# Strassen's seven block products for the third of four matrix layers, in a kernel of block attention and two MLPs on one core

## The chip, the core and the metric

The kernel runs on one core of one Trainium2 chip. The core has a matrix engine (TensorE, PE in the profile; PEld are its weight loads), a vector engine (VectorE, DVE), an activation engine (ScalarE, ACT), GpSimd (POOL) and a queue engine (SyncE, SP) that issues the transfers between HBM and SBUF, the on-chip memory of 128 partitions. Matmuls write to PSUM, eight banks of 128 x 512 float32. The metric is device time of one execution in microseconds (us), as the median of several runs.

## The reference

Attention over a band and block summaries gives x of 1536 tokens x 512; a gated MLP and a squared-ReLU MLP follow. The four matrix layers below are 512 x (2 x 1536), 1536 x 512, 512 x 2048 and 2048 x 512; q, k, v are 2 x 8 x 768 x 64.

```python
def reference(**kwargs):
    ...
    attn_out = _attn_ref(**attn_kwargs)
    B, H, S, D = attn_out.shape
    x = np.ascontiguousarray(attn_out.transpose(0, 2, 1, 3)).reshape(B * S, H * D)
    x = _moe_ref(x=x, **moe_kwargs)
    return _moe2_ref(x=x, **moe2_kwargs)

def _moe_ref(x, w_gate, w_val, w_out):
    g = x @ w_gate                          # layer one, with val
    silu = g * (1.0 / (1.0 + np.exp(-g)))
    val = x @ w_val
    return (silu * val @ w_out)             # layer two

def _moe2_ref(x, w_in, w_out):
    h = np.maximum(x @ w_in, 0.0)           # layer three
    return (h * h @ w_out)                  # layer four
```

## The kernel before

**Precision.** Every operand of the four layers is kept as two tiles of the format float32r, a high part (a ScalarE cast) and a low part (VectorE: the value less the high part), and each product is three matmuls, high x high, high x low and low x high (`ORDER`). The weights arrive as float64 words; ScalarE and VectorE convert them to float32 once (`convert`), a float32 copy is kept in HBM (`kept1`, `kept2`, `kept34`), and later passes load that.

**Tiling and stages.** The tokens are cut into 3 sets of 512 (`TS`). After a prologue with the first set's attention, a list of `periods` is worked off in order: 36 periods "12" (3 sets x 12 column tiles of 128 of layer one, each with one tile of layer two), then 48 periods "34" (3 sets x 16 column tiles of layer three, each with one tile of layer four). Period k multiplies the column tile of layer one or three into a bank of `ps_m` (two banks), and behind it `second` does layer two or four for the tile of period k-1, into four banks of `ps_c` that accumulate over a whole set. A period "12" has 24 + 12 matmuls of 512 columns, a period "34" has 12 (L538, `multiply3`: weights stationary, 512 tokens moving) + 12 (L557: 128 tokens of h stationary, 512 columns of the fourth weight moving).

**Work beside it.** In a period "34" ScalarE takes relu (L751) and square (L752), VectorE the square in float32 and the low part (L753, L754); both split the weights of the next period (`split_chunk`, L224 and L225). Attention of sets 1 and 2 is laid into the periods of the sets ahead by hand (`place`, with the tables `first`, `after` and `late`, three steps to a period: step 3k + j). The conversion of the third and fourth weights (`background`) runs in the periods of sets 1 and 2, 7/6 steps of it per step. When a set of layer two is complete, its four banks are split into x2 (L565, L566).

**Order.** All of it is written in program order under a manual schedule: each engine works through its own instructions strictly in that order and waits on semaphores. Buffers come from pools (`x_p`, `h_p`, `t_p`, `wr_p`, `wf_p`, `ws_p`, and `const` and `att_p` for attention); a tile's first writer waits until the buffer's previous tile has been read. SyncE issues the loads in order too.

## Time and profile before

| what | us |
|---|---|
| median of 3 runs (lowest, highest) | 643.67 (643.62, 645.46) |
| the profiled execution, its own time | 643.53 |
| its span, first to last instruction | 641.8 |
| TensorE, VectorE, ScalarE busy in it | 630.0, 427.0, 344.0 |
| the 48 periods "34" and the tail of layer two (373.67 to 637.00) | 263.33 |
| the last set of periods "12" (275.83 to 373.67) | 97.84 |

The span is one profiled execution; the runs are timed without a profile. Busy times are of each engine alone and lie beside each other; matmuls overlap in the records, so that a busy TensorE says nothing yet about the interval between two of them.

### The profile page before, as it was taken

The page shows a single profiled execution, that of the slowest core. Times are in us where ns is not written, and L with a number is a line of the kernel's source. Part 1 is how long each engine was busy: PE and PEld are TensorE (multiplying, and loading weights), DVE is VectorE, ACT ScalarE, POOL GpSimd, SP SyncE. Part 2 cuts the span into 40 slices and gives each one's busy share as a digit, 9 for nine tenths or more (in the row PEclk, how much of TensorE's full clock was granted, in tenths as well). Part 3 has the DMA queues.
Part 4 walks back from the last instruction along what each step waited for, and adds up shares of the span by engine and source line. Part 5 has one row for each costly group of instructions (what it writes and reads, how often), then busy time and mean ns, then how long its engine had stood idle before and what let it go on. Part 6 is the DMA issues. An engine that isn't in the chain of part 4 may idle for free.

```text
span 641.8 us, 8650 instructions
## 1 busy us (share of the span) xinstructions
PE 630.0 (98%) x3176; PEld 515.7 (80%) x3176; DVE 427.0 (67%) x519; ACT 344.0 (54%) x623; POOL 25.8 (4%) x41
## 2 busy tenths in 40 slices
PE   8889999999999999999999999999999999999997
PEld 6657788877888888888888888888888888888885
DVE  5999999997577776777767664444454444544443
ACT  3683877884466887554444344444444444444442
POOL 3411000000000000000000000000000000000000
PEclk9899999999999999999999999999999999999999
DMA  8999999747984965766755333222252222432311
GB/s 341 320 371 369 361 328 357 260 170 242 369 249 128 338 203 203 245 246 234 254 201 189 123 117 113 99 96 96 73 182 92 91 95 99 162 101 99 100 50 65
DMA packets 51995, 125.62 MB, mean 196 GB/s; under 512 B 8304, under 2 KB 15216, under 8 KB 50416
## 3 DMA queue, kind: packets, MB, share of 16 engines
q1 hardware_dynamic: 51952, 125.06, 57.1%
q8 instruction: 25, 0.41, 0.3%
q14 instruction: 18, 0.15, 0.1%
HBM read 103.28 MB, written 20.97 MB: 194 GB/s over the span
## 4 chain that ended last, share of the span: by engine, by line
PE 92%; DVE 4%; ACT 2%; issue 1%; POOL 0%; POOLq 0%; DVEq 0%
PE bank L529 29%; PE bank L557 20%; PE bank L538 20%; PE bank L555 15%; PE bank L362 2%; PE bank L465 2%; PE bank L449 1%; PE bank L277 1%; ACT s L393 1%; PE bank L375 1%; DVE wlo L225 1%; DVE wf L188 1%; DVE ks L346 0%; PE bank L370 0%; DVE m L382 0%
## 5 line engine op out<-in xcount | busy, mean ns | idle before, releaser
L225 DVE TENSOR_TENSOR wlo<-wf,whi 128x1024 fp32r<-128x1024 f32 (+2 forms) x85 | 122.1, 1436 | 48.6 <-ACT whi L224 47.9
L224 ACT CAST whi<-wf 128x1024 fp32r<-128x1024 f32 (+2 forms) x85 | 104.1, 1225 | 79.3 <-PE bank L557 54.2
L529 PE MATMUL bank<-xh,whi 128*128 128x512 f32 x288 | 115.8, 402 | 0.0
L529 PE MATMUL bank<-xh,wlo 128*128 128x512 f32 x288 | 112.8, 392 | 2.1 <-DVE wlo L225 2.1
L529 PE MATMUL bank<-xl,whi 128*128 128x512 f32 x288 | 112.6, 391 | 0.6 <-DVE xl L476 0.6
L753 DVE TENSOR_TENSOR r<-r 128x512 f32<-128x512 f32 x48 | 33.2, 692 | 89.2 <-ACT hh L752 89.2
L751 ACT ACTIVATE r<-bank 128x512 f32<-128x512 f32 x48 | 28.7, 598 | 87.6 <-PE bank L538 87.6
L557 PE MATMUL bank<-whi,hl 128*128 128x512 f32 x192 | 74.8, 390 | 0.0
L557 PE MATMUL bank<-whi,hh 128*128 128x512 f32 x192 | 74.7, 389 | 0.0
L557 PE MATMUL bank<-wlo,hh 128*128 128x512 f32 x192 | 74.7, 389 | 0.0
L538 PE MATMUL bank<-xh,whi 128*128 128x512 f32 x192 | 74.7, 389 | 0.0
L538 PE MATMUL bank<-xl,whi 128*128 128x512 f32 x192 | 74.7, 389 | 0.0
L538 PE MATMUL bank<-xh,wlo 128*128 128x512 f32 x192 | 74.7, 389 | 0.0
L529 PEld LDWEIGHTS bank<-xh,wlo 128*128 128x128 f32 x288 | 54.0, 188 | 14.8 <-DVE wlo L225 3.4
L739 ACT CAST hh<-g 128x512 fp32r<-128x512 f32 x36 | 22.2, 617 | 77.9 <-DVE g L738 77.9
L529 PEld LDWEIGHTS bank<-xh,whi 128*128 128x128 f32 x288 | 54.1, 188 | 12.0 <-ACT g L736 0.7
L529 PEld LDWEIGHTS bank<-xl,whi 128*128 128x128 f32 x288 | 54.1, 188 | 11.8 <-DVE xl L476 1.3
L555 PE MATMUL bank<-hh,whi 128*128 128x512 f32 x144 | 57.2, 397 | 0.0
L555 PE MATMUL bank<-hh,wlo 128*128 128x512 f32 x144 | 56.1, 390 | 0.0
L555 PE MATMUL bank<-hl,whi 128*128 128x512 f32 x144 | 56.1, 389 | 0.0
L557 PEld LDWEIGHTS bank<-whi,hl 128*128 128x128 f32 x192 | 36.0, 188 | 7.8 <-DVE hl L754 0.3
L557 PEld LDWEIGHTS bank<-whi,hh 128*128 128x128 f32 x192 | 36.0, 188 | 7.6
(87 smaller groups left out, 899.4 us busy)
## 6 DMA issues: line engine op xcount, KB each, us to landing
wf<-kept SPq DMA_DIRECT2D x120, 256.0 KB
raw<-in_w_dram SPq DMA_DIRECT2D x44, 512.0 KB
...
```

Source lines behind the costliest of these rows:

```text
L188: nc.vector.scalar_tensor_tensor(out=w, in0=hw, scalar=0xC0000000, in1=w, op0=ALU.bitwise_and, op1=ALU.bitwise_or)
L224: lambda: nc.scalar.copy(hi[:, cs], t),
L225: lambda: nc.vector.tensor_sub(lo[:, cs], t, f32(hi[:, cs])),
L362: nc.tensor.matmul(ps[:, i * W:(i + 1) * W], self.q[:, j * UB + i, :], self.kw[j][:, i, 0:W], start=True, stop=True,)
L465: nc.tensor.matmul(ps[r, at + i * QB:at + (i + 1) * QB], self.v[:, j * UB + i, r], a[:, i * P + h * QB:i * P + (h + 1) * QB], start=True, ...
L529: nc.tensor.matmul(p, w[a][:, c], x[i][kk], start=(kk == 0 and n == 0), stop=(kk == KD - 1 and n == 2),)
L538: nc.tensor.matmul(p, w[a][:, c], x[i][kk], start=(kk == 0 and n == 0), stop=(kk == KD - 1 and n == 2),)
L555: nc.tensor.matmul(ps[t], w[a][:, c], h[e], start=(f == 0 and n == 0), stop=(f == last and n == 2))
L557: nc.tensor.matmul(ps[t], h[e][:, t * P:(t + 1) * P], w[a][:, off:off + DM], start=(f == 0 and n == 0), stop=(f == last and n == 2),)
L739: nc.scalar.copy(h[0], g)
L751: nc.scalar.activation(r, p, ACTF.Relu)
L753: nc.vector.tensor_mul(r, r, r)
```

## The change

Layer three is worked in 2 passes of 768 tokens (`NG`), each with 8 steps (`NB`) of 256 columns of its weight; step p takes two neighbouring column tiles. A step is a product of 2 x 2 blocks: tokens in two halves of 384 (`TB`), the 512 inputs in two halves of 256, the columns in two of 128. It is done by seven products of blocks in Winograd's form of Strassen's method, in place of eight: m1 to m7 (`block(p, n)`), each 2 x 3 matmuls of 384 columns, from four weight sums (`sums34`: t1 to t4) and four token sums (`operands`: s1 to s4 in the usual naming, here `s3`, `a21`, `a21`, `s4`). The sums of products (`u2`, `u3`, `sum_up`) give the four blocks of the output; `sum_up` squares the positive part, `high34` and `low34` split it, and `fourth` multiplies layer four for step p-1 into six banks (four of `ps_c`, two of `ps_a`). The order inside a step alternates products and parts of layer four (`rest(0)` to `rest(3)`); in step 0 the rest is what is left of layer two.

Tokens and weights of the seven products are summed in float32 and then split: x2 stays float32 (`put_x2` copies, nothing is split there). The sums and splits of the first pass's tokens are laid into steps 76 on of the third set of layer one, those of the second pass into steps 1 to 8 of the first (`ready`). The float32 weights of a step are loaded two steps ahead (`load34`). Attention's pools sit at the other end of SBUF and are closed after step 72, and their place becomes `xo_p`; the raw words' pools are closed four steps ahead of layer three and become `wr34`. The conversion of the third and fourth weights runs at 9/7 steps per step.

```diff
+    att_c, raw_c = ExitStack(), ExitStack()
+    const = att_c.enter_context(tc.tile_pool(name="const", bufs=1, side="right"))
+    att_p = att_c.enter_context(tc.tile_pool(name="att", bufs=1, side="right"))
...
+    x_p = ctx.enter_context(tc.tile_pool(name="x", bufs=6))
...
+    wr_p = raw_c.enter_context(tc.tile_pool(name="wr", bufs=3))
+    vn_p = raw_c.enter_context(tc.tile_pool(name="vn", bufs=2))
...
-    def multiply3(p, w, x):
-        for kk in range(KD):
-            c = slice(kk * P, (kk + 1) * P)
-            for n, (a, i) in enumerate(ORDER):
-                nc.tensor.matmul(
-                    p, w[a][:, c], x[i][kk],
-                    start=(kk == 0 and n == 0), stop=(kk == KD - 1 and n == 2),
...
-
...
+
+    def second(f, w, off, h, ts):
...
-        last = (F1 if kind == "12" else F2) - 1
-        for t in range(4):
+            acc[:] = [bank(ps_c) for _ in range(4)]
+        for t in ts:
...
-        for t in range(4):
-            if kind == "12":
-                nc.scalar.copy(x2[0][t], ps[t])
-                nc.vector.tensor_sub(x2[1][t], ps[t], f32(x2[0][t]))
-            else:
...
+                nc.tensor.matmul(acc[t], w[a][:, c], h[e], start=(f == 0 and n == 0), stop=(f == F1 - 1 and n == 2))
...
+    TB = 384
+    HK = KD // 2
+    NG = B * S // (2 * TB)
+    NB = F2 // 2
...
+    def put_x2(i, t):
...
+        pieces.sort(key=lambda p: p[0] - p[1])
+        for copy, (a, e) in zip((nc.scalar.copy, nc.vector.tensor_copy), pieces):
+            n = a // TB
+            if n not in x2:
+                x2[n] = x_p.tile([P, KD, TB], F32, tag="x", name="x2")
+            copy(x2[n][:, t, a - n * TB:e - n * TB], acc[t][:, a - i * TS:e - i * TS])
+
...
+    def operands(g):
+        (a11, a12), (a21, a22) = ([x2[2 * g + t][:, k * HK:(k + 1) * HK, :] for k in range(2)] for t in range(2))
+        d = x_p.tile([P, KD, TB], F32, tag="x", name="dx")
+        s3, s4 = d[:, 0:HK, :], d[:, HK:KD, :]
+
+        def hi(n, src):
+            xo[g, n] = xo_p.tile([P, 2, HK, TB], F32R, tag="o", name="o", bufs=9)
+            nc.scalar.copy(xo[g, n][:, 0, :, :], src)
+
+        def lo(n, src):
+            nc.vector.tensor_sub(xo[g, n][:, 1, :, :], src, f32(xo[g, n][:, 0, :, :]))
+
+        def split(n, src):
+            return [lambda: hi(n, src), lambda: lo(n, src)]
+
+        sub, add = nc.vector.tensor_sub, nc.vector.tensor_add
+        return (
+            split(0, a11)
+            + [lambda: sub(s3, a11, a21), lambda: add(a21, a21, a22)]
+            + split(4, a21)
+            + [lambda: sub(a21, a21, a11), lambda: sub(s4, a12, a21)]
+            + split(5, a21) + split(2, s4) + split(6, s3) + split(3, a22) + split(1, a12)
+        )
+
+    BLK = HK * P
+    OF = (("bb", 0), ("bb", 1), ("b2", 0), ("t4", 1), ("tt", 0), ("tt", 1), ("t4", 0))
...
+    f_34, w3_t, w4_t, h_t = {}, {}, {}, {}
+
+    def load34(p, j):
+        pool, tag = (wr34, "f") if p % 2 and j else (wf_p, "wf")
+        t = f_34[p, j] = pool.tile([P, CC], F32, tag=tag, name="wf")
+        nc.sync.dma_start(out=t[:, 0:2 * C2], in_=kept34[2 * (p % NB) + j][:, :])
+
+    def sums34(p):
+        f1, f2 = f_34[p, 0], f_34[p, 1]
+        b11, b21, b12, b22 = (f[:, k * BLK:(k + 1) * BLK] for f in (f1, f2) for k in range(2))
+        t1, t2, t3, t4 = (f[:, (4 + k) * BLK:(5 + k) * BLK] for f in (f1, f2) for k in range(2))
+        sub = nc.vector.tensor_sub
+        return [lambda: sub(t1, b12, b11), lambda: sub(t2, b22, t1), lambda: sub(t3, b22, b12), lambda: sub(t4, b21, t2)]
+
+    def source34(p, tag):
+        j, a, n = {"bb": (0, 0, 2), "tt": (0, 4, 2), "b2": (1, 1, 1), "t4": (1, 4, 2)}[tag]
+        return f_34[p, j][:, a * BLK:(a + n) * BLK], n * BLK
+
+    def hi3(p, tag):
+        src, n = source34(p, tag)
+        t = w3_t[p, tag] = wr34.tile([P, 2, n], F32R, tag=tag, name=tag, bufs=2 if tag in ("bb", "t4") else 1)
...
+    def lo3(p, tag):
+        src, n = source34(p, tag)
+        t = w3_t[p, tag]
+        nc.vector.tensor_sub(t[:, 1, :], src, f32(t[:, 0, :]))
...
+    def hi4(p, j):
+        if j == 0:
+            w4_t[p] = tuple(ws_p.tile([P, CC], F32R, tag=f"w{e}", name=f"w4{e}") for e in ("hi", "lo"))
...
+    def lo4(p, j):
+        c = slice(j * DM, (j + 1) * DM)
+        nc.vector.tensor_sub(w4_t[p][1][:, c], f_34.pop((p, j))[:, C2:2 * C2], f32(w4_t[p][0][:, c]))
+
+    def block(p, n, pool=ps_m):
+
+        g, (tag, half) = p // NB, OF[n]
+        w, x = w3_t[p, tag], xo[g, n]
+        ps = bank(pool)
+        for k in range(HK):
+            c = slice(half * BLK + k * P, half * BLK + (k + 1) * P)
+            for i, (a, e) in enumerate(ORDER):
+                nc.tensor.matmul(
+                    ps[:, 0:TB], w[:, a, c], x[:, e, k, :], start=(k == 0 and i == 0), stop=(k == HK - 1 and i == 2)
+                )
+        return ps[:, 0:TB]
...
+    def snap(ps, tag):
+        t = part(tag)
+        nc.scalar.copy(t, ps)
+        return t
...
+    def sum_up(a, other):
+        t = t_p.tile([P, TB], F32, tag="t", name="c")
+        nc.vector.tensor_add(t, a, other)
+        nc.vector.scalar_tensor_tensor(out=t, in0=t, scalar=0.0, in1=t, op0=ALU.max, op1=ALU.mult)
+        return t
+
+    def high34(p, n, c):
+        nc.scalar.copy(new_h34(p, n)[:, 0, :], c)
+
+    def low34(p, n, c):
+        nc.vector.tensor_sub(h_t[p, n][:, 1, :], c, f32(h_t[p, n][:, 0, :]))
...
+    def fourth(p, n):
+
+        g, m = divmod(p, NB)
+        if m == 0 and n == 0:
+            acc[:] = [bank(ps_c) for _ in range(4)] + [bank(ps_a) for _ in range(2)]
+        f, t = 1 - n // 2, n % 2
+        h, w = h_t.pop((p, n)), w4_t[p]
+        for j in range(3):
+            for i, (a, e) in enumerate(ORDER):
+                nc.tensor.matmul(
+                    acc[3 * t + j], h[:, e, j * P:(j + 1) * P], w[a][:, f * DM:(f + 1) * DM],
+                    start=(m == 0 and n < 2 and i == 0), stop=(m == NB - 1 and n >= 2 and i == 2),
+                )
...
+        def attention_done():
+            nonlocal xo_p
+            att_c.close()
+            xo_p = ctx.enter_context(tc.tile_pool(name="xo", bufs=1, side="right"))
+            for j, f in enumerate(operands(0)):
+                at(late, 76 + j + j // 3, f)
+
...
+        e = 3 * len(periods)
+        at(first, 6 * F1, attention_done)
+        at(late, e - 6, lambda: load34(0, 0))
+        at(late, e - 4, lambda: load34(0, 1))
+        at(late, e - 4, words_done)
+        at(late, e - 3, lambda: [f() for f in sums34(0)])
+        for n, tag in ((3, "bb"), (3, "tt"), (2, "b2"), (2, "t4")):
+            at(late, e - n, lambda tag=tag: hi3(0, tag))
+            at(late, e - n, lambda tag=tag: lo3(0, tag))
+        at(late, e - 1, lambda: load34(1, 0))
+        at(late, e - 1, lambda: load34(1, 1))
...
-                if F1 <= k < K34:
-                    ticks += 7
-                    while ticks >= 6:
+                if k >= F1:
+                    ticks += 9
+                    while ticks >= 7:
                         next(bg, None)
-                        ticks -= 6
-
...
+        for p in range(NG * NB + 1):
...
+            if live:
+                spare = ps_m if p else ps_a
+                m1, m5 = block(p, 0), block(p, 4)
+                if more:
+                    for f in sums34(p + 1):
+                        f()
+            rest(0)
+            if live:
+                s1, s5 = snap(m1, "s1"), snap(m5, "s5")
+                if p:
+                    high34(p - 1, 2, c2)
+                    low34(p - 1, 2, c2)
+                prepare(0)
+                hi4(p, 0)
+                hi4(p, 1)
+                m6, m7 = block(p, 5, spare), block(p, 6, spare)
+                lo4(p, 0)
+                lo4(p, 1)
+            elif p:
+                high34(p - 1, 2, c2)
+                low34(p - 1, 2, c2)
+            rest(1)
+            if live:
+                u2, u3 = (h_p.tile([P, TB], F32, tag=t, name=n) for t, n in (("hh", "u2"), ("hl", "u3")))
+                nc.vector.tensor_add(u2, m6, s1)
+                nc.vector.tensor_add(u3, m7, u2)
+                nc.vector.tensor_add(u2, u2, s5)
+                if more:
+                    hi3(p + 1, "bb")
+                c = sum_up(u3, s5)
+                high34(p, 1, c)
+                if more:
+                    lo3(p + 1, "bb")
+                low34(p, 1, c)
+                prepare(1)
+                if p == 0:
+                    put_x2(bi, 0)
+                    put_x2(bi, 1)
+                if p + 2 < NG * NB:
+                    load34(p + 2, 0)
+                    load34(p + 2, 1)
+                m3, m4 = block(p, 2), block(p, 3)
+                if more:
+                    hi3(p + 1, "tt")
+                    lo3(p + 1, "tt")
+            rest(2)
+            if live:
+                c = sum_up(m3, u2)
+                high34(p, 0, c)
+                c2 = sum_up(m4, u3)
+                low34(p, 0, c)
+                high34(p, 3, c2)
+                low34(p, 3, c2)
+                prepare(2)
+                if p == 0:
+                    put_x2(bi, 2)
+                    put_x2(bi, 3)
+                m2 = block(p, 1, spare)
+                if more:
+                    hi3(p + 1, "b2")
+                    lo3(p + 1, "b2")
+                    hi3(p + 1, "t4")
+            rest(3)
+            if live:
+                c2 = sum_up(m2, s1)
+                if more:
+                    lo3(p + 1, "t4")
```

Two places show how instructions move. On TensorE, before, the end of a period "34" and the start of the next look like this (`whi`, `wlo` are the two parts of a weight tile, `xh`, `xl` of the tokens, `hh`, `hl` of h):

```order
L538 MATMUL bank_5288<-xh3_3465,whi_5246 128x512
L538 MATMUL bank_5288<-xl3_3469,whi_5246 128x512
L538 MATMUL bank_5288<-xh3_3465,wlo_5247 128x512
L557 MATMUL bank_4801<-whi_5246,hh_5248 128x512
L557 MATMUL bank_4801<-whi_5246,hl_5249 128x512
L557 MATMUL bank_4801<-wlo_5247,hh_5248 128x512
```

In the changed kernel, in the middle of step 5, between two of layer four's parts (`o` is a split token operand, `tt`, `t4`, `b2`, `bb` are split weight blocks or sums, `h34` a split block of h):

```order
L666 MATMUL bank_3609<-w4lo_4065,h34_4103 128x512
L666 MATMUL bank_3610<-w4hi_4064,h34_4103 128x512 x2
L666 MATMUL bank_3610<-w4lo_4065,h34_4103 128x512
L628 MATMUL bank_4258<-o_3093,b2_4156 128x384 x6
L628 MATMUL bank_4265<-o_3202,t4_4159 128x384 x6
L666 MATMUL bank_3605<-w4hi_4064,h34_4208 128x512 x2
L666 MATMUL bank_3605<-w4lo_4065,h34_4208 128x512
```

Where twelve matmuls of 512 columns stood behind twelve of another layer, groups of six with 384 columns stand in ones or twos between groups of nine of layer four.

On VectorE, before, a period "34" is three instructions (here two periods' worth, the weight split `wlo` between square and split of h):

```order
L754 TENSOR_TENSOR hl_5249<-r_5267,hh_5248 128x512
L225 TENSOR_TENSOR wlo_5285<-wf_5226,whi_5284 128x1024
L753 TENSOR_TENSOR r_5303<-r_5303 128x512
L754 TENSOR_TENSOR hl_5287<-r_5303,hh_5286 128x512
L225 TENSOR_TENSOR wlo_5321<-wf_5265,whi_5320 128x512
```

In the changed kernel step 0 begins like this, up to the copies of x2 (`wf` are the loaded weights and their sums, `u2`, `u3` and `c` the sums of products, `bank` a product in PSUM, `s1`, `s5` copies of m1 and m5):

```order
L595 TENSOR_TENSOR wf_3456<-wf_3458,wf_3456 128x256 x2
L595 TENSOR_TENSOR wf_3458<-wf_3458 128x256
L595 TENSOR_TENSOR wf_3458<-wf_3456 128x256
L618 TENSOR_TENSOR w4lo_3489<-wf_3353,w4hi_3488 128x512
L618 TENSOR_TENSOR w4lo_3489<-wf_3384,w4hi_3488 128x512
L932 TENSOR_TENSOR u2_3511<-bank_3492,s1_3484 128x384
L933 TENSOR_TENSOR u3_3512<-bank_3499,u2_3511 128x384
L934 TENSOR_TENSOR u2_3511<-u2_3511,s5_3486 128x384
L647 TENSOR_TENSOR c_3518<-u3_3512,s5_3486 128x384
L648 SCALAR_TENSOR_TENSOR c_3518<-c_3518 128x384
L609 TENSOR_TENSOR bb_3516<-wf_3456,bb_3516 128x512
L655 TENSOR_TENSOR h34_3521<-c_3518,h34_3521 128x384
```

Ahead of the first sum that reads a product, VectorE now has four weight sums and two splits of the fourth weight; behind these three rows of u the sum and square of one block, a weight split and a split of h, and only behind all of it, with the copies of x2 and the split `tt`, the sum that reads m3 and gives its bank back (the next row, `c` from a bank and `u2`).

## Rows read from the trace of the kernel before

Durations in rows of the timeline are us, in grouped rows the last number ahead of the second bar is the mean in ns; a bracket or an arrow names what ended the idle time before.

**Rows 1.** The page, part 1: busy us, share of the span, instructions.

```profile
span 641.8 us, 8650 instructions
...
PE 630.0 (98%) x3176; PEld 515.7 (80%) x3176; DVE 427.0 (67%) x519; ACT 344.0 (54%) x623; POOL 25.8 (4%) x41
```

**Rows 2.** Stretches (us): busy us of each engine (instructions), granted clock, DMA share, GB/s.

```profile
275.83:373.67 97.84, 97.84 (x433) 81.04 (x432) 68.69 (x74) 41.17 (x47) 0.00 (x0) 1.00 0.55 191
373.67:637.00 263.33, 263.33 (x1163) 217.84 (x1162) 130.13 (x154) 114.37 (x155) 0.00 (x0) 1.00 0.30 101
```

**Rows 3.** Groups by form, TensorE: xcount, busy us, mean ns of one.

```profile
L538 PE MATMUL bank<-xh,whi 128*128 128x512 f32 x192 | 74.7, 389 | 0.0
...
L557 PE MATMUL bank<-whi,hh 128*128 128x512 f32 x192 | 74.7, 389 | 0.0
...
L362 PE MATMUL bank<-kw,q 128*128 128x120 f32 x128 | 16.2, 275 | 0.3 <-POOL kw L354 0.3
```

**Rows 4.** Timeline, TensorE, one period of layers three and four: start, duration.

```profile
400.95 0.39 PE L538 MATMUL bank<-xh,whi 128*128 128x512 f32 x1
...
401.17 0.39 PE L538 MATMUL bank<-xl,whi 128*128 128x512 f32 x1
...
406.39 0.39 PE L538 MATMUL bank<-xh,whi 128*128 128x512 f32 x1
```

**Rows 5.** Timeline, TensorE, prologue: 480 columns and what follows.

```profile
15.85 0.38 PE L370 MATMUL bank<-xl,xh 128*128 128x480 f32 x1
16.06 1.05 PE L375 MATMUL bank<-kw,q 128*128 128x120 f32 x8
```

**Rows 6.** Timeline, TensorE, attention: eight matmuls of 120 columns.

```profile
119.99 1.04 PE L362 MATMUL bank<-kw,q 128*128 128x120 f32 x8
```

**Rows 7.** Groups by form, TensorE's weight loads: those of line 362.

```profile
L362 PEld LDWEIGHTS bank<-kw,q 128*128 128x128 f32 x128 | 16.0, 191 | 1.5 <-POOL kw L354 0.7
```

**Rows 8.** Groups by form, VectorE: two-input operations of 1024, 512 and 256.

```profile
L225 DVE TENSOR_TENSOR wlo<-wf,whi 128x1024 fp32r<-128x1024 f32 x49 | 60.0, 1225 | 40.5 <-ACT whi L224 40.5
...
L753 DVE TENSOR_TENSOR r<-r 128x512 f32<-128x512 f32 x48 | 33.2, 692 | 89.2 <-ACT hh L752 89.2
...
L476 DVE TENSOR_TENSOR xl<-bank,xh 128x256 fp32r<-128x256 f32 x8 | 3.1, 415 | 0.0
```

**Rows 9.** Timeline, VectorE, end of layer two.

```profile
378.02 0.69 DVE L753 TENSOR_TENSOR r<-r 128x512 f32<-128x512 f32 x1 [1.95 <-ACT hh L752]
378.75 0.69 DVE L754 TENSOR_TENSOR hl<-r,hh 128x512 fp32r<-128x512 f32 x1
379.36 2.48 DVE L566 TENSOR_TENSOR xl<-bank,xh 128x512 fp32r<-128x512 f32 x4
```

**Rows 10.** Groups by form, ScalarE: casts of 1024, reads of PSUM of 512.

```profile
L224 ACT CAST whi<-wf 128x1024 fp32r<-128x1024 f32 x49 | 51.7, 1055 | 55.2 <-PE bank L557 53.0 <-PE bank L555 2.2
...
L751 ACT ACTIVATE r<-bank 128x512 f32<-128x512 f32 x48 | 28.7, 598 | 87.6 <-PE bank L538 87.6
```

**Rows 11.** Timeline, ScalarE, end of layer two.

```profile
377.89 2.08 ACT L565 CAST xh<-bank 128x512 fp32r<-128x512 f32 x4
```

**Rows 12.** Timeline, all engines: a matmul's end and its reader's start.

```profile
419.76 0.39 PE L538 MATMUL bank<-xh,wlo 128*128 128x512 f32 x1
...
420.19 0.60 ACT L751 ACTIVATE r<-bank 128x512 f32<-128x512 f32 x1 [1.89 <-PE bank L538]
```

**Rows 13.** Timeline, SyncE's queue: loads of weights in the last token set.

```profile
325.99 2.92 SPq L166 DMA_DIRECT2D wf<-kept  x4
```

**Rows 14.** Timeline, ScalarE: the copy that waited for one of these loads.

```profile
332.96 1.49 ACT L224 CAST whi<-wf 128x1536 fp32r<-128x1536 f32 x1 [0.77 <-DMA wf<-kept]
```

**Rows 15.** Stretches of the prologue: granted clock behind the engines.

```profile
10.60:20.80 10.20, 8.19 (x45) 5.79 (x45) 7.32 (x17) 7.19 (x37) 3.52 (x7) 1.00 1.03 418
20.80:24.30 3.50, 3.50 (x17) 3.25 (x17) 3.37 (x7) 0.46 (x1) 1.64 (x2) 0.51 1.02 260
```

**Rows 16.** Timeline, TensorE, prologue: idle time before the half clock.

```profile
19.47 0.48 PE L370 MATMUL bank<-xh,xh 128*128 128x480 f32 x1 [1.75 <-ACT s L393]
```

188 lines of the change are left out of this document (94 added, 94 removed).

## Prediction

> **What bounds the kernel now.** I read the engines' busy shares first, then stretches, then single intervals. TensorE is busy for 98% of a span of 641.8 us, VectorE for 67%, ScalarE for 54% [rows 1]. The view by stretches cuts out the two parts that matter here: the last 512 tokens of the first MLP (97.84 us) and then the second MLP, layers three and four (263.33 us, with the tail of layer two). In both TensorE is busy without a break at the full granted clock; VectorE has 70% and 49% there [rows 2]. So in the changed stage the end is set by how many matmuls TensorE issues and at what interval.
>
> The durations in the grouped view do not give that interval: 192 matmuls of a kind last 389 ns each [rows 3], and the 1152 of the stage at that length would need 448 us. They overlap. The timeline has the interval: two matmuls of 512 columns start 0.22 to 0.23 us apart, and one period of the stage (one of the 48 pairs of token set and column tile, 24 matmuls) goes from 400.95 to 406.39, so 5.44 us or 0.2267 us each [rows 4]. The stage is 48 x 5.44 = 261.2 us.
>
> **What the change takes from TensorE.** Layer three had 3 x 16 x 4 x 3 = 576 matmuls of 512 columns. It now has, in each of 16 steps (2 passes of 768 tokens, 8 pairs of column tiles), 7 products x 2 x 3 = 42 matmuls of 384 columns, 672 in all. Layer four keeps 576 of 512 columns. No matmul of 384 columns is in the trace. Near it stands one of 480 columns, whose successor starts 0.21 us later [rows 5], against 0.2267 for 512. In proportion to its columns a matmul of 384 would take 0.170 us; if what 0.2267 has over 512 columns at 2.4 GHz (0.2133) is a fixed 0.0133 us, it is 0.1733. I take 0.1717. The loading of weights must also keep that pace: eight matmuls of 120 columns, each with its own load of 128, are through in 1.04 us with the last one's 0.275 in it [rows 3, 6], so 0.109 us apart, though one such load is recorded as 191 ns [rows 7]; it is below 0.17.
> Sum: 672 x 0.1717 = 115.4 us in place of 576 x 0.2267 = 130.6, so **15.2 us less** (13.9 to 16.3 by the two ways to price it).
> The Trainium skill, TensorE: Matmul & The Clock Gate, "Back-to-back issue gap", gives N/2.4 ns and 2.5 ns more for a warm matmul, 215.8 ns for 512. The trace differs by 11 ns: 226.7. By the page 384 columns are 162.5 ns, an estimate by which layer three would be 109.2 us and 21.4 us would be saved.
>
> **What it adds beside TensorE.** VectorE ops of 256, 512 and 1024 elements last 0.415, 0.692 and 1.225 us with two inputs [rows 8]; 384 lies between at 0.554, 768 at 0.958 and 128 at 0.29. Independent ones follow closer than they last (four of 512 in 2.48 us, 0.60 each), dependent ones 0.04 us after the end (378.02 + 0.69 to 378.75) [rows 9]. In one step VectorE now does 4 sums of weights and a split of 256 elements, 5 splits of 512, and 15 operations of 384 (three sums u, four times sum and square, four splits of h): 2.1 + 3.5 + 8.3 = 13.9 us as recorded, about 12.5 with the overlap of those that do not hang on their predecessor. A step has 42 x 0.1717 + 36 x 0.2267 = 15.37 us of TensorE to hide it, where before VectorE was busy for half the time. ScalarE (5 casts of 512, one of 256, 6 of 384) needs some 6.6 us by its 1.055 for 1024 and 0.598 for 512 from PSUM [rows 10] and a pace of 0.50 [rows 11]: no bound.
>
> I laid the instructions of the three engines end to end in their program order with these durations, 0.04 us from an engine's end to the next one's start (a matmul at 419.76 lasts to 420.15, its reader starts at 420.19 [rows 12]) and 0.2 us back to TensorE. A regular step has no wait for TensorE. Two places have.
> *The first step.* It has 12 matmuls of layer two in place of 36 of layer four, so 42 x 0.1717 + 12 x 0.2267 = 9.93 us, and all of VectorE's work and four copies of x2. Its first weight sums need the second step's words, whose load goes into the buffer that the last weight split of layer two frees; that split stands behind five operations for the first step's weights and ends some 2 us ahead of the stage. The row of four issues that end at 328.91 and the copy that waited for one of them until 332.96 give 4.0 us for a landing [rows 13, 14]; so the words are there 2.0 to 2.5 us into the stage. VectorE then goes through sums, splits and u in the order shown above; u3 cannot start before the product m7 ends at 5.5. The sum that reads m3, and with it frees the bank of the second step's first product, ends at 11.0 and TensorE wants the bank at 9.93: 1.25 us of wait with the 0.2. What VectorE is late then shows as waits of 0.7, 0.2 and 0.4 us for other banks within step 1; 2.5 us together.
> *The change of passes.* The second pass's tokens are summed and split during the first: 12 operations of 768, of which five (4.8 us) fall in steps 7 and 8. There VectorE has 14 to 15.5 us and is late for two banks by 1.3 us.
> That makes 3.9 us. If each VectorE operation took 0.03 us less, the waits add up to 2.1 us, with 0.07 more to 9.2.
>
> **What else moves.** In the last token set of layer one the first pass's 12 operations of 768 (11.5 us) and a conversion of the words that goes 9/7 steps at a time and not 7/6 (VectorE some 0.3 us more in a period of 36 x 0.2267 = 8.16) come to VectorE's 68.69 busy us of 97.84 [rows 2]; 84 of 97.84 are still under the time. I put 0 to 1 us on it, 0.5 in the sum. If that cover is gone, the next to be late is the weight split that layer one waits for. The loads are 1 MB in 15.4 us, where the stage moved 101 GB/s before [rows 2]: hidden. The end of the kernel is as before, copies of the last banks and their transfers out; of six banks four are copied while layer four still runs: 0.
> The clock: TensorE's granted clock fell to half (0.51, so 1.2 GHz) from 20.8 to 24.3 us [rows 15], after an idle time of 1.75 us up to 19.47 [rows 16]. The waits in step 1 are shorter, one by one. I leave it out of the sum; if it came, 3.5 us at half would cost up to 1.75.
>
> **Sum.** -15.2 + 3.9 + 0.5 = -10.8 us. The profiled execution took 643.53 us, its span 641.8 and 1.7 around it; the median of the runs is 643.67. **643.5 - 10.8 = 632.7, so 633 us.**
>
> **Rivals.**
> *VectorE becomes the bound of each step (slower).* Its 25 operations last 13.9 us as recorded. If none overlapped, each 0.04 us after its predecessor's end, that is 14.9 of 15.37 us, and since it also stands still for each product, TensorE would wait in every step. From 0.1 us more for each operation on than I took, all of the gain is eaten: the waits reach 15.4 us and the steps 1 to 6 take 16.2 us each; with 0.15 us more it is 32 us of waits, 643.5 - 15.2 + 32 + 0.5 = 661. For it: 49% becomes some 85% in strictly ordered work. Against it: the four of 512 that followed each other in 0.60 us each, beside a busy TensorE.
> The Trainium skill, VectorE: DVE Perf Modes, "The DRAIN you can't avoid", has this as a rule: after each operation the pipe empties before the next starts, and the number of operations is what to keep low. By that rule the 14.9 us would hold; the trace's four at 0.60 for a recorded 0.69 do not follow it, the dependent pair does.
> *The weight loads set the interval (slower).* If a matmul's load could not be closer than the recorded 0.191 us, 672 x 0.191 = 128.4 us would take the gain of 15.2 down to 2.2, and with the waits it is 645.7; if the interval stayed at 0.2267 whatever the columns, the 96 additional matmuls cost 21.8 us and it is 668. Against both: 0.109 and 0.21 above.
> *The waits do not come (faster still).* VectorE then keeps ahead also in step 0, because the words land earlier: 628; with a shorter interval of 384 columns down to 624.
>
> **How the numbers follow.** My case 0.67, from 628 (16.3 saved, 1 us of waits) to 640 (13.9 saved, 9.2 of waits, 0.5, and up to 1.2 of the clock); VectorE as the bound 0.14 (from 641 on); weight loads 0.07; no waits 0.12. The range 627 to 642 leaves out the two slow rivals for the most part and little of the fast one. Within 0.3% (1.9 us) of before, about what can be told from no change here, lies part of the first two rivals: same 0.08, slower 0.13, faster 0.79.
>
> **What would show it.** Right: products of 384 columns start 0.170 to 0.174 us apart; TensorE's steps of 15.4 us with waits named VectorE (the sum that frees a bank) in the first two steps and at the change of passes, and next to none between; VectorE busy for some 85% of the stage; the last set of layer one as long as before. Wrong: waits for VectorE in every step, the interval at 0.19 or above, a half clock after the first step, or weight splits late in layer one.

## The result and the profile after

The changed kernel takes 633.91 us (median of 4 runs, 632.96 to 634.9) against 643.64 (643.61 to 645.46) in the same session: ratio 0.9842, 95% interval 0.9816 to 0.9868. Predicted were 633, with 627 to 642 as range. The profiled execution took 632.96 us, the sum of the prediction 632.7.

The page, part 1, answers to [rows 1]: 96 more matmuls in 14.6 us less of TensorE, and VectorE from 67% to 82%.

```profile
span 631.3 us, 9062 instructions
...
PE 615.4 (97%) x3272; PEld 522.9 (83%) x3272; DVE 519.7 (82%) x794; ACT 337.2 (53%) x686; POOL 25.1 (4%) x41
```

The two stretches of [rows 2], in the same columns: the last set of layer one is as long as before with 7.4 us more of VectorE in it, the second MLP shorter, VectorE busy for 84% of it, TensorE for all but 2.3 us (a record of a matmul is longer than the interval to the next, so idle time comes out smaller than the 3.8 us of waits that the lengths of the steps give below).

```profile
275.50:373.30 97.80, 97.80 (x433) 81.03 (x432) 76.10 (x88) 46.82 (x58) 0.00 (x0) 1.00 0.53 188
373.30:627.00 253.70, 251.36 (x1261) 226.57 (x1260) 213.64 (x411) 102.22 (x209) 0.00 (x0) 1.00 0.19 70
```

From the first product of layer three (373.42) to the start of the last matmul of layer four (627.15) it is 253.73 us; between the same two points it was 263.79. These 10.06 us are nearly the whole 10.5 by which the span fell (641.8 to 631.3); the stage begins 0.33 us earlier, which is less than the 2.2 us by which that moment differs between executions.

TensorE's timeline, first of a regular step (the start of m1, m5, and of the next step's m1), then m2 of step 0 and m1 of step 1, and last the waits that are left in steps 1 and 8:

```profile
401.22 1.21 PE L628 MATMUL bank<-o,bb 128*128 128x384 f32 x6
402.27 1.20 PE L628 MATMUL bank<-o,tt 128*128 128x384 f32 x6
...
416.69 1.21 PE L628 MATMUL bank<-o,bb 128*128 128x384 f32 x6
```

```profile
382.40 1.21 PE L628 MATMUL bank<-o,bb 128*128 128x384 f32 x6
384.55 1.29 PE L628 MATMUL bank<-o,bb 128*128 128x384 f32 x6 [0.94 <-DVE c L647]
```

```profile
389.23 1.31 PE L628 MATMUL bank<-o,tt 128*128 128x384 f32 x6 [0.27 <-ACT s L638]
398.03 1.31 PE L628 MATMUL bank<-o,bb 128*128 128x384 f32 x6 [0.18 <-DVE c L647]
...
495.51 1.29 PE L628 MATMUL bank<-o,tt 128*128 128x384 f32 x6 [0.28 <-DVE c L647]
507.77 1.29 PE L628 MATMUL bank<-o,bb 128*128 128x384 f32 x6 [0.67 <-DVE c L647]
```

Six matmuls of 384 columns start 1.04 to 1.05 us ahead of the next six; from one matmul of 384 columns to what follows it is 0.173 us in the median of the stage and 0.174 in the mean, and I count with 0.1735. A regular step lasts 15.47 us. At 384.55 step 1's first product starts 2.15 us after m2 began, so 1.1 us late; the wait is put down to a sum of VectorE. The wait for ScalarE in step 1 goes back to VectorE too: ScalarE's copy `s` had itself waited for a sum (row below). VectorE's timeline names the sum at the end of step 0, and what VectorE did since the words came:

```profile
375.83 1.56 DVE L595 TENSOR_TENSOR wf<-wf 128x256 f32<-128x256 f32 x4 [1.66 <-DMA wf<-kept]
...
383.24 0.69 DVE L609 TENSOR_TENSOR tt<-wf,tt 128x512 fp32r<-128x512 f32 x1 [0.23 <-ACT tt L604]
383.85 0.55 DVE L647 TENSOR_TENSOR c<-bank,u 128x384 f32<-128x384 f32 x1
384.43 0.56 DVE L648 SCALAR_TENSOR_TENSOR c<-c 128x384 f32<-128x384 f32 x1
```

```profile
388.70 0.86 ACT L638 COPY s<-bank 128x384 f32<-128x384 f32 x2 [0.52 <-DVE c L647]
```

The words land 2.4 us into the stage, and the sum that frees the bank ends at 384.40, 11.0 us into it: both as predicted. Operations of 384 last what was taken (0.554), by the grouped view (rows of 366 to 640 us):

```profile
L648 DVE SCALAR_TENSOR_TENSOR c<-c 128x384 f32<-128x384 f32 x64 | 35.7, 558 | 2.2
L655 DVE TENSOR_TENSOR h<-c,h 128x384 fp32r<-128x384 f32 x64 | 35.6, 557 | 18.0 <-ACT h L652 17.5
```

The view by stretches, columns as in [rows 2], has step 1, a regular step and step 8. VectorE is busy for 16.1 us in step 1 and 16.2 in step 8, more than a regular step lasts:

```profile
384.50:401.20 16.70, 16.20 (x78) 13.91 (x79) 16.06 (x34) 8.47 (x19) 0.00 (x0) 1.00 0.17 64
416.70:432.20 15.50, 15.50 (x80) 14.09 (x79) 13.70 (x27) 5.82 (x12) 0.00 (x0) 1.00 0.19 69
494.00:510.90 16.90, 15.95 (x79) 13.95 (x78) 16.21 (x31) 10.14 (x20) 0.00 (x0) 1.00 0.29 109
```

### The profile page after: what moved, and what is told of

Read it like the earlier page. It is cut to its first block, busy times and chain, and to the rows that moved or that the text cites. A ratio compares the mean times of both kernels' runs of the same rounds, so it can differ in the third digit from the quotient of the medians.

```text
span 631.3 us, 9062 instructions
## 1 busy us (share of the span) xinstructions
PE 615.4 (97%) x3272; PEld 522.9 (83%) x3272; DVE 519.7 (82%) x794; ACT 337.2 (53%) x686; POOL 25.1 (4%) x41
## 4 chain that ended last, share of the span: by engine, by line
PE 87%; DVE 6%; DMA 4%; ACT 1%; issue 1%; POOL 0%; SPq 0%; ACTq 0%; DVEq 0%; POOLq 0%
PE bank L519 30%; PE bank L666 18%; PE bank L628 16%; PE bank L533 15%; PE bank L352 2%; PE bank L267 2%; PE bank L455 2%; DMA kept<-wf 1%; PE bank L439 1%; DMA vn<-in_vN_dram 1%; DMA raw<-in_w_dram 1%; DVE c L647 1%; PE bank L365 1%; DVE c L648 1%; DVE o L567 1%
## 5 line engine op out<-in xcount | busy, mean ns | idle before, releaser
L666 PE MATMUL bank<-w4hi,h 128*128 128x512 f32 x384 | 118.4, 390 | 0.0
L519 PE MATMUL bank<-xh,whi 128*128 128x512 f32 x288 | 115.8, 402 | 0.0
L519 PE MATMUL bank<-xh,wlo 128*128 128x512 f32 x288 | 112.8, 392 | 1.7 <-DVE wlo L215 1.7
L519 PE MATMUL bank<-xl,whi 128*128 128x512 f32 x288 | 112.6, 391 | 0.6 <-DVE xl L466 0.6
L666 PEld LDWEIGHTS bank<-w4hi,h 128*128 128x128 f32 x384 | 71.3, 188 | 10.3
L666 PE MATMUL bank<-w4lo,h 128*128 128x512 f32 x192 | 74.7, 389 | 0.0
L215 DVE TENSOR_TENSOR wlo<-wf,whi 128x1536 fp32r<-128x1536 f32 (+2 forms) x37 | 63.2, 1708 | 6.8 <-ACT whi L214 4.8
L214 ACT CAST whi<-wf 128x1536 fp32r<-128x1536 f32 (+2 forms) x37 | 53.4, 1443 | 23.5 <-DVE wf L183 14.8
L519 PEld LDWEIGHTS bank<-xh,wlo 128*128 128x128 f32 x288 | 54.1, 188 | 13.9 <-DVE wlo L215 2.6
L178 DVE SCALAR_TENSOR_TENSOR wf<-raw,wf 128x1024 uint32<-128x1024 uint32 (+2 forms) x29 | 40.8, 1406 | 0.3
L183 DVE SCALAR_TENSOR_TENSOR wf<-raw,wf 128x1024 uint32<-128x1024 uint32 (+2 forms) x29 | 40.8, 1407 | 0.1
L628 PE MATMUL bank<-o,bb 128*128 128x384 f32 x192 | 38.9, 339 | 1.8 <-DVE c L647 1.8
```

Of the source, the lines that this page charges most:

```text
L178: nc.vector.scalar_tensor_tensor(out=w, in0=hw, scalar=0xC0000000, in1=w, op0=ALU.bitwise_and, op1=ALU.bitwise_or)
L183: nc.vector.scalar_tensor_tensor(out=w, in0=lw, scalar=29, in1=w, op0=ALU.logical_shift_right, op1=ALU.bitwise_or)
L214: lambda: nc.scalar.copy(hi[:, cs], t),
L215: lambda: nc.vector.tensor_sub(lo[:, cs], t, f32(hi[:, cs])),
L519: nc.tensor.matmul(p, w[a][:, c], x[i][kk], start=(kk == 0 and n == 0), stop=(kk == KD - 1 and n == 2),)
L628: nc.tensor.matmul(ps[:, 0:TB], w[:, a, c], x[:, e, k, :], start=(k == 0 and i == 0), stop=(k == HK - 1 and i == 2))
```

## The experiments

I read the steps of the stage from each trace (from one step's first product to the next's), since what lies ahead of the stage differs by up to 2.2 us from execution to execution (its first product starts between 372.8 and 375.1 us). "Stage" runs from the first product of layer three to the start of layer four's last matmul. The second run of the changed kernel is `after_again`. Times are medians of four or five executions for the changed kernel, after_again, e7_pool_both, e8_order and e9_order2, and of a single one for the others. The stage and the steps are those of one traced execution. For e7_pool_both that is the slowest of its five (639.46 us).

| kernel | time, us | stage | step 0 | 1 | 2 to 6 | 7 | 8 | 9 to 14 |
|---|---|---|---|---|---|---|---|---|
| changed | 633.91 | 253.73 | 11.13 | 16.68 | 15.47 | 15.47 | 16.92 | 15.47 |
| after_again | 632.98 | 253.77 | 11.11 | 16.71 | 15.47 | 15.47 | 16.95 | 15.47 |
| e1_early | 633.18 | 253.71 | 11.11 | 16.68 | 15.47 | 15.47 | 16.91 | 15.47 |
| e2_eight | 647.50 | 268.31 | 11.17 | 17.72 | 16.51 | 16.51 | 16.91 | 16.51 |
| e3_halves | 663.41 | 284.29 | 12.28 | 17.77 | 17.59 | 17.59 | 17.59 | 17.59 |
| e5_dve2 | 638.82 | 257.94 | 12.34 | 17.93 | 15.47 | 15.80 | 18.33 | 15.47 |
| e5_dve4 | 649.27 | 270.63 | 13.64 | 19.14 | 16.4 | 17.49 | 19.57 | 15.7 to 16.1 |
| e6_pool_sums | 635.44 | 255.36 | 11.54 | 16.28 | 15.88, 15.47 | 16.65 | 16.95 | 15.47 |
| e6_pool_x | 636.76 | 257.33 | 11.11 | 16.70 | 15.47 | 16.16 | 19.83 | 15.47 |
| e7_pool_both | 636.64 | 258.39 | 11.54 | 16.27 | 15.47 | 16.16 | 20.88 | 15.47 |
| e8_order | 631.58 | 252.47 | 10.03 | 16.77 | 15.47 | 15.47 | 16.67 | 15.47 |
| e8_dve2 | 636.19 | 256.44 | 10.91 | 18.07 | 15.47 | 15.47 | 18.46 | 15.47 |
| e9_order2 | 632.31 | 252.33 | 10.03 | 17.67 | 15.47 | 15.47 | 15.64 | 15.47 |

**Is the gain the eighth product?** One product, m2, is computed a second time into its bank, the second time from the start, so that layer three has eight products to pay for again.

```diff
-        for k in range(HK):
+        for k in times * list(range(HK)):
...
-                m2 = block(p, 1, spare)
+                m2 = block(p, 1, spare, 2)
```

> An eighth product: m2 is computed twice into the same bank, the second time over the first, everything else as in the changed kernel; so each step has 48 matmuls of 384 columns as eight products of blocks would. Theory (the gain is the seventh of layer three's matmuls, at 0.1735 us each, less the waits): 96 x 0.1735 = 16.7 us more, of which the waits at step 1 and step 8 swallow about 2, so 633.0 + 14.6 = 647.6, which is above the 643.6 of before. Rival (the gain is from what the passes of 768 tokens save beside TensorE: fewer splits, loads and periods): well under 643, most of the gain stays.

It took 647.5 us, and the regular steps 16.51, 1.04 more: six matmuls at 0.1733. TensorE's timeline, the start of two steps:

```profile
402.24 1.21 PE L628 MATMUL bank<-o,bb 128*128 128x384 f32 x6
...
418.75 1.21 PE L628 MATMUL bank<-o,bb 128*128 128x384 f32 x6
```

So the missing product is what the change gains, and it is paid at the interval of 384 columns. In steps 0 and 8 next to nothing was added (11.17 for 11.13, 16.91 for 16.92), since the additional product lies in the wait that is there anyway. With eight products the stage is 268.31 us, 4.5 longer than before: what else the change brings costs time, and the missing product alone pays.

**What sets the interval?** Each matmul of 384 columns becomes two of 192, each with its own weight load.

```diff
-        for k in range(HK):
+        for s in (slice(0, TB // 2), slice(TB // 2, TB)):
+            for k in range(HK):
...
-                    ps[:, 0:TB], w[:, a, c], x[:, e, k, :], ...
+                        ps[:, s], w[:, a, c], x[:, e, k, s], ...
```

> Each matmul of 384 columns of layer three as two of 192, so 1344 matmuls with 1344 weight loads, the same result. Theory (an interval is the columns at 2.4 GHz and a fixed 0.0133 us): 1344 x 0.0933 = 125.4 us in place of 116.6, of which the waits swallow up to 2: 640 to 642. Rival (from here on the load of the weights sets the interval, at the 0.109 to 0.112 us that eight matmuls of attention show): 1344 x 0.110 = 147.8 us, so about 663. If the recorded 0.19 us of a load were its interval, 1344 x 0.19 = 255 us and 770.

663.41 us: my figure fell, the rival's held. TensorE's timeline of this kernel, one product and what follows:

```profile
399.96 1.48 PE L629 MATMUL bank<-o,bb 128*128 128x192 f32 x12
401.28 0.65 PE L667 MATMUL bank<-w4hi,h 128*128 128x512 f32 x2
```

Twelve in 1.32 us are 0.110 each (0.112 by the regular step, 17.59 us with 84 of them and 36 of 512), not the 0.0933 that 192 columns and a fixed 0.0133 would be. It is the pace of [rows 6], where matmuls of 120 columns were 0.109 apart: pairs of a load and a matmul follow each other at about 0.11 us here whether the matmul has 120 or 192 columns. Whether it is the load that sets this pace is not shown, since no run has these matmuls without their loads. The 0.1735 of 384 columns lies well above it, so the rival of the prediction by which loads set the interval does not apply to the change itself; blocks half as wide would meet this pace.

**Are the late words the cause of the first waits?** The first step's sums, and the splits of its first pairs, are moved one place ahead, so that the buffer for step 1's words comes free earlier.

```diff
-        at(late, e - 3, lambda: [f() for f in sums34(0)])
+        at(after, e - 3, lambda: [f() for f in sums34(0)])
...
-            at(late, e - n, lambda tag=tag: hi3(0, tag))
-            at(late, e - n, lambda tag=tag: lo3(0, tag))
+            at(after if n == 3 else late, e - n, lambda tag=tag: hi3(0, tag))
+            at(after if n == 3 else late, e - n, lambda tag=tag: lo3(0, tag))
```

> In the changed kernel VectorE waits 1.66 us in step 0 for the second step's words, and TensorE then waits 0.94 us for a bank at the start of step 1. Here the sums and splits of the first step's weights are issued ahead of the activation of the last period, so that layer two's last weight split ends some 2.4 us earlier and the words of step 1 are there when the stage begins. Theory (VectorE's amount of work in step 0 sets the wait; the words only come in a gap that two casts of ScalarE and the product m7 leave anyway): the first two steps stay at 27.8 us together, within 0.3. Rival (the late words set it): they lose 1.1 to 1.6 us and the execution goes from 633.0 to about 631.6.

VectorE's timeline at the start of the stage (373.65 here) shows the sums 0.5 us into it in place of 2.4, without a wait for the words, and a new wait right behind:

```profile
374.12 1.55 DVE L595 TENSOR_TENSOR wf<-wf 128x256 f32<-128x256 f32 x4
376.96 0.69 DVE L618 TENSOR_TENSOR w4lo<-wf,w4hi 128x512 fp32r<-128x512 f32 x1 [1.30 <-ACT w4hi L614]
```

Steps 0 and 1 together are 27.79 us for 27.81. The late words cost nothing: what VectorE gains by them it spends waiting for ScalarE's cast (1.30) and then for m7 (0.48); the sum that frees the bank ends 11.0 us into the stage as before.

**How much room has VectorE?** Two and four additions of 384 columns more on VectorE in each step, which nothing reads.

```diff
+                for _ in range(4):          # 2 in e5_dve2
+                    nc.vector.tensor_add(u2, s1, s5)
                 nc.vector.tensor_add(u2, m6, s1)
```

> VectorE gets four more sums of 384 elements in each step, ahead of u2, which are overwritten by the real u2: 2.3 us more in a step of 15.47. Theory (VectorE has some 2 us to spare in a regular step and is late where it has more to do): past the point where it decides; regular steps go to 16.2 us, the sum of TensorE's waits from 3.9 to about 18 us, the execution to about 647. Rival (VectorE is far off the path between the two places): only the first two steps and step 8 grow, by 2 us each, and the execution is below 640. Rival (VectorE bounds every step already): each step grows by the whole 2.3 us, 633 + 37 = 670.

> Two extra additions of 384 columns on VectorE per step (work left over that nothing reads), half of the four of the run before, which lengthened the stage by 16.9 us. My theory: VectorE still has about 1 us to spare in a regular step (two additions are 1.1 us), so regular steps stay at 15.45 to 15.5 us; only the steps in which VectorE also has the sums of the words or the second pass's splits get longer: steps 0 and 1 together by about 2.4 us, step 8 by about 1.4. Stage +3.9 us, time about 637. Rival (what VectorE is given goes into the time in proportion, so that it bounds every step already): half of 16.9, stage +8.4 us spread over all steps, regular steps about 16.0, time about 641.5.

With two (1.1 us) regular steps stay at 15.47 and the stage is 4.2 us longer, 2.5 of it in steps 0 and 1 and 1.4 in step 8: theory 3.9, rival 8.4. With four (2.2 us) regular steps grow too, to 16.4 in the first pass and 15.7 to 16.1 in the second, the stage by 16.9 us in all. So VectorE has between 1.1 and 2.2 us to spare in a regular step and none in steps 0, 1 and 8. The run with four took 2.3 us more than expected; steps 0, 1, 7 and 8 are longer by 2.0 to 2.7 us each. It shows one thing more, in TensorE's timeline and the view by stretches (columns as in [rows 2]):

```profile
386.46 1.94 PE L628 MATMUL bank<-o,bb 128*128 128x384 f32 x5 [3.45 <-DVE c L647]
```

```profile
372.00:385.20 13.20, 11.01 (x59) 10.06 (x57) 10.82 (x23) 5.07 (x11) 0.00 (x0) 1.00 0.40 154
385.20:392.20 7.00, 5.74 (x17) 5.38 (x18) 6.74 (x15) 4.19 (x10) 0.00 (x0) 0.51 0.00 0
392.20:400.00 7.80, 7.64 (x40) 6.73 (x39) 7.42 (x16) 1.25 (x3) 0.00 (x0) 1.00 0.38 138
```

The wait for the bank has grown to 3.45 us, and the granted clock is at half (1.2 GHz) around its end and for some 7 us in all. That this cost time is not shown: step 1, where most of it lies, is 2.46 us longer than in the changed kernel, and step 0, nearly all of it at the full clock, 2.51.

**Can GpSimd take VectorE's work?** GpSimd stands idle in this stage. It gets the four sums of the words, then the low halves of the second pass's tokens, then both.

```diff
-        sub = nc.vector.tensor_sub
+        sub = nc.gpsimd.tensor_sub              # e6_pool_sums, e7_pool_both
...
-            nc.vector.tensor_sub(xo[g, n][:, 1, :, :], src, f32(xo[g, n][:, 0, :, :]))
+            (nc.gpsimd if g else nc.vector).tensor_sub(...)   # e6_pool_x, e7_pool_both
```

> The four subtractions of 256 columns that make the words' sums of each step of layers three and four go from VectorE to GpSimd, which is idle in this stage. My theory: VectorE loses about 1.7 us of work per step; steps 1 and 8, which are longer than the others because VectorE is late in them, get shorter by about 0.5 and 0.8 us, the wait of about 1.2 us at step 1's first product stays (the casts of step 0 are ahead of it either way), regular steps stay at 15.47. Stage -1.3 us, time about 631.7 to 632.0. Rival: GpSimd is slow (its 480-column operation in the stage of layers one and two took 1.05 us) or holds VectorE up while both work, the sums land later and casts and weights wait for them: stage the same or longer, time 633 or more.

> The low halves of the second pass's token blocks (made around step 8) go from VectorE to GpSimd; the words' sums stay on VectorE. My theory: the wait at the change of passes (step 8 is 1.45 us longer than a regular step) is VectorE's extra work of the splits, so it goes: step 8 at 15.5 to 15.7 us, all else unchanged, stage -1.2 to -1.45 us, time about 631.6. Rival: the wait belongs to the change of passes itself (the accumulators of layer four being put out, or the banks), or GpSimd is later with the splits than VectorE: step 8 stays at 16.9 us or grows, time 633 or more.

> Both moves to GpSimd at once, the words' sums and the second pass's low splits. My theory: step 1 shorter by 0.5 us and step 8 by 1.4 us, the 1.2 us of wait at the first product of step 1 stays: stage -1.8 to -2.0 us, time about 631 to 631.3, faster than the changed kernel by 0.3%. Rival: GpSimd is the late engine now (sums and splits one after the other on it around step 8), the gain of one move is given back by the other: time 632 to 634.

All three are slower in the stage, by 1.6, 3.6 and 4.7 us (the last in the slowest of five executions, with the granted clock at 0.82 in the stretch from 510 to 514 us); with both moves the time is 636.64 us, 0.9878 of before (0.9858 to 0.9898). My theory fell. TensorE's added waits are not put down to GpSimd in any of the three: nearly all are waits for VectorE's sum that reads a bank (L647). GpSimd's timeline of e6_pool_sums (four sums with VectorE idle, then four beside VectorE's work) and VectorE's show why:

```profile
366.02 2.94 POOL L595 TENSOR_TENSOR wf<-wf 128x256 f32<-128x256 f32 x4 [146.61 <-DMA wf<-kept]
...
383.90 4.00 POOL L595 TENSOR_TENSOR wf<-wf 128x256 f32<-128x256 f32 x4 [3.19 <-DVE x L553]
```

```profile
384.06 1.12 DVE L609 TENSOR_TENSOR tt<-wf,tt 128x512 fp32r<-128x512 f32 x1 [0.23 <-ACT tt L604]
385.10 0.54 DVE L647 TENSOR_TENSOR c<-bank,u 128x384 f32<-128x384 f32 x1
385.68 0.56 DVE L648 SCALAR_TENSOR_TENSOR c<-c 128x384 f32<-128x384 f32 x1
...
387.21 1.57 DVE L655 TENSOR_TENSOR h<-c,h 128x384 fp32r<-128x384 f32 x2
```

While GpSimd works, the split of 512 takes 1.12 us and not 0.69, two splits of 384 take 1.57 and not 1.22 (the same two in the changed kernel, at 385.97), and the sum that has one input in a bank takes its 0.54. The square, which reads one tile twice, takes its 0.56; GpSimd's own sums take 1.00 us each there, against 0.73 with VectorE idle. Over the stage, in the grouped view, first of the changed kernel and then of e6_pool_sums:

```profile
L595 DVE TENSOR_TENSOR wf<-wf 128x256 f32<-128x256 f32 x63 | 23.8, 420 | 2.2 <-DMA wf<-kept 1.7
...
L609 DVE TENSOR_TENSOR tt<-wf,tt 128x512 fp32r<-128x512 f32 x16 | 11.1, 691 | 0.2 <-ACT tt L604 0.2
```

```profile
L595 POOL TENSOR_TENSOR wf<-wf 128x256 f32<-128x256 f32 x64 | 63.9, 1018 | 305.1 <-DMA wf<-kept 240.0 <-DVE bb L609 42.3 <-DVE c L647 10.5
```

```profile
L655 DVE TENSOR_TENSOR h<-c,h 128x384 fp32r<-128x384 f32 x64 | 44.6, 708 | 24.4 <-ACT h L652 24.0
...
L609 DVE TENSOR_TENSOR tt<-wf,tt 128x512 fp32r<-128x512 f32 x16 | 16.2, 1010 | 0.2 <-ACT tt L604 0.2
...
L647 DVE TENSOR_TENSOR c<-bank,u 128x384 f32<-128x384 f32 x32 | 17.6, 549 | 0.0
```

Taken off VectorE were 23.8 us of sums (23.0 of them behind 373.3). Its busy time fell by only some 5 us (from 214.06 to 209.22 between 373.3 and 640), mostly because the splits of `h` took 9 us more (708 for 557 ns) and those of `tt` 5 (1010 for 691). The sums also end later: what the later words cost and what the held-up splits cost is not told apart by a run. In e6_pool_x the same is seen with longer operations: a split `tt` lasts 1.93 us beside GpSimd's 1.86:

```profile
488.78 1.86 POOL L567 TENSOR_TENSOR o<-x,o 128x768 fp32r<-128x768 f32 x1 [39.54 <-ACT o L564]
```

```profile
489.26 1.93 DVE L609 TENSOR_TENSOR tt<-wf,tt 128x512 fp32r<-128x512 f32 x1 [0.70 <-ACT tt L604]
491.11 0.54 DVE L647 TENSOR_TENSOR c<-bank,u 128x384 f32<-128x384 f32 x1
```

The Trainium skill, SBUF — State Buffer, "Who interferes with whom", states this: a VectorE instruction with two inputs in SBUF contends with a GpSimd instruction that reads SBUF; one with at most one such input, outside VectorE's modes that use two ports, does not. The rows agree for the splits (0.69 to 1.12 and 1.93) and for the sum that reads a bank (0.54 unchanged). The square, two reads of one tile, was not lengthened here (558 ns in the mean of the stage in both kernels).

**Order or amount?** The same work in another order on VectorE: in each step the sums that free the banks of m3, m4 and m2 go ahead of the low halves of the next step's words, of the second pass's splits and of the copies of x2. Then the same with two additional additions, and the changed kernel once more.

```diff
-                prepare(1)
-                if p == 0:
-                    put_x2(bi, 0)
-                    put_x2(bi, 1)
+                prepare_hi(1)
...
                     hi3(p + 1, "tt")
-                    lo3(p + 1, "tt")
             rest(2)
...
                 c2 = sum_up(m4, u3)
+                prepare_lo()
+                if more:
+                    lo3(p + 1, "tt")
+                if p == 0:
+                    put_x2(bi, 0)
+                    put_x2(bi, 1)
...
                 c2 = sum_up(m2, s1)
+                prepare_lo()
+                if p == 0:
+                    put_x2(bi, 2)
+                    put_x2(bi, 3)
                 if more:
+                    lo3(p + 1, "b2")
                     lo3(p + 1, "t4")
```

> The same work on the same engines, in another order on VectorE alone: in each step the sums that free a bank of layer three (m3, m4, m2) stand ahead of the low halves of the next step's words, of the second pass's splits and of the copies of the outgoing tokens in steps 0 and 1; ScalarE's order stays but for the second pass's casts. My theory: the 3.9 us of waits are banks freed late by VectorE, not missing work of VectorE over a whole step, so they shrink: step 0 from 11.13 to 10.0 to 10.3 us, steps 1 and 8 from 16.7 and 16.9 to 15.6 to 16.2 us, regular steps stay at 15.47; stage -1.5 to -2.5 us, time about 631. Rival (VectorE is behind by an amount of work in steps 0, 1, 7 and 8, whatever the order): what is put behind the sums is late in its turn and the waits move to the low halves, stage within 0.5 us of 253.9, time about 633.

> The new order with the two extra additions of 384 columns on VectorE per step (nothing reads them). With the old order they cost the stage 4.2 us. If order is what made VectorE late, they cost the new order less than 2 us, time about 632 to 633. If it is the amount of work, they cost 4 us or more again, time 635 to 637.

> The changed kernel itself, beside the two above on the same chip, so that a difference of 0.3% can be told: 633 to 635 us, stage 253.7 to 254.0 us.

The changed kernel took 632.98 us here (632.44 to 633.56; 0.9826 of before, 0.9804 to 0.9848), the new order 631.58 (631.3 to 632.2; 0.9803, 0.9782 to 0.9824). The stage is 1.3 us shorter, between theory (1.5 to 2.5) and rival (under 0.5), and the time is what the theory gave (about 631). The wait ahead of step 1's first product is gone, step 0 is 10.03 us, and TensorE's timeline shows what took its place:

```profile
385.91 0.97 PE L628 MATMUL bank<-o,tt 128*128 128x384 f32 x4 [0.43 <-DVE tt L609]
388.60 0.70 PE L666 MATMUL bank<-w4hi,h 128*128 128x512 f32 x2 [0.33 <-DVE x L553]
```

```profile
507.17 1.14 PE L628 MATMUL bank<-o,bb 128*128 128x384 f32 x5 [0.94 <-DVE o L567]
```

They are the very operations that were put behind the sums: the low half of `tt`, the copies, and in step 8 the split of the token block that m2 reads. Two additional additions cost this order 4.0 us again, as the rival said, and not under 2.

**The new order mended.** In step 8 the split goes ahead again, the low half of `tt` stands between the additions and the squares, the copies ahead of m2's sum. The edit is against the first new order:

```diff
-                c = sum_up(m3, u2)
-                high34(p, 0, c)
-                c2 = sum_up(m4, u3)
-                prepare_lo()
+                if p == NB:
+                    prepare_lo()
+                c, c2 = sum_up(m3, u2, True), sum_up(m4, u3, True)
                 if more:
                     lo3(p + 1, "tt")
+                square(c)
+                high34(p, 0, c)
+                square(c2)
+                prepare_lo()
...
-                c2 = sum_up(m2, s1)
-                prepare_lo()
                 if p == 0:
                     put_x2(bi, 2)
                     put_x2(bi, 3)
+                c2 = sum_up(m2, s1)
+                prepare_lo()
```

> The new order, with what the trace of the first one showed late put right: in step 8 the split of the last token block, on which m2 waited 0.94 us, stands ahead of the sums again; the low halves of the next step's second pair of blocks stand between the additions that free the banks of m3 and m4 and the squares; the copies of the outgoing tokens in step 1's stretch stand ahead of m2's sum. My theory (waits are VectorE's order as long as what is put back is not wanted at once): step 0 stays at 10.0 us, step 1 from 16.8 to 15.5 to 16.2, step 8 from 16.7 to 15.5 to 15.8, regular steps 15.47; stage 250.7 to 252.0 us against 252.7 and 254.0, time 629.6 to 630.9. Rival (amount of work in steps 0, 1 and 8): step 1 or the steps behind it take over the wait, stage 252.5 to 254, time 631.5 to 633.

632.31 us (631.58 to 632.57), 0.9817 of before (0.9801 to 0.9833). Step 8 fell to 15.64 us as expected: there the wait was order. TensorE's timeline, the start of step 8 and of step 9:

```profile
494.64 1.21 PE L628 MATMUL bank<-o,bb 128*128 128x384 f32 x6
...
510.28 1.21 PE L628 MATMUL bank<-o,bb 128*128 128x384 f32 x6
```

Steps 0 and 1 together are 27.70 against 26.80 in the first new order and 27.81 in the changed kernel: there the rival held. The stage, 252.33, lies between the ranges of theory (250.7 to 252.0) and rival (252.5 to 254). VectorE's timeline of this kernel shows that part of step 1's wait is of my making:

```profile
386.19 0.67 DVE L553 COPY x<-bank 128x128 f32<-128x128 f32 x2 [0.49 <-ACT x L553]
386.78 1.02 DVE L659 TENSOR_TENSOR h<-c,h 128x384 fp32r<-128x384 f32 x2
388.19 0.67 DVE L553 COPY x<-bank 128x128 f32<-128x128 f32 x2 [0.39 <-ACT x L553]
```

Its copies of x2 wait for ScalarE's, which now stand behind a cast that waits for VectorE's later square. The first new order with this one's step 8 would, by the table, have a stage near 251.4 us; it was not tried. In time the first new order lies 0.2% below the changed kernel of the same session, with executions that do not overlap (631.3 to 632.2 against 632.44 to 633.56). In the stage, where two executions of the changed kernel agree within 0.04 us, both orders are 1.3 to 1.4 us shorter.

## Why the prediction was right, by its steps

*The interval* was the term that was mis-sized: 0.1735 us for 384 columns and not 0.1717, at the upper of the two prices. 672 x 0.1735 = 116.6, so 14.0 us less and not 15.2.

*The waits*, predicted as 3.9 us (2.5 in the first two steps, 1.3 at the change of passes), are 1.1, 1.2 and 1.45 us by the lengths of steps 0, 1 and 8 against 10.0 (42 x 0.1735 + 12 x 0.2267) and 15.47, so 3.8. The words, the sum that ends 11.0 us into the stage, and the banks, two of them in step 8, are those that were named. (The 0.2 us from a sum's end back to TensorE, for which the prediction gave no row, are 0.15 here, 384.40 to 384.55.) One reason in this step was not needed: the prediction let the words' landing start the chain, but with the words there (e1_early) the waits are the same. What makes them is VectorE's work in these steps and its order (e5_dve2, e8_order): of step 8's wait 1.3 of 1.45 us were order (e9_order2). How much of step 1's is amount of work stays open, since the order that would tell it was spoilt by ScalarE's copies.

*Layer one* was given 0.5 us and took none: 97.80 us, at 76.10 busy us of VectorE where the prediction counted 84. It counted 12 operations of 768 for a pass where the kernel has 11 (10.5 us), and more of the conversion in this set where there is less: 30 operations of 1024 in place of 34, 29.2 us for 33.0.

Together: -14.0 + 3.8 = -10.2 for the stage, where 10.06 were measured; 1.2 too much gain, and against it 0.5 too much for layer one and 0.1 for the waits, so the sum of -10.8 came out within 0.7. That the profiled execution came still closer (632.96 for 632.7; the median is 633.91) is luck: the moment at which the stage begins alone differs by 2.2 us from execution to execution.

*The rivals.* VectorE is not the bound of each step: 12 of the 14 steps from 1 to 14 are 15.47 us, but it stands only 1.1 to 2.2 us from it, and with four operations more it is. The pace of load and matmul, 0.11 us, does not set the interval at 384 columns, and does at 192. The waits did come, 3.8 us of them. The granted clock stayed at 1.00 in the stage. Three figures of the prediction do not follow from the terms that it names, and none enters its sum of -10.8: its upper price saves 14.1 us and not 13.9, which it uses for the bound of 640; an interval of 0.2267 gives 665.8 us without waits and 669.7 with them, for 668; and 0.170, the shortest interval that it prices from rows, gives 627.7 without waits, for 624.
